# Three loads of an attention-plus-MLP kernel cut by lanes: 96 lanes and four times 8

## The chip, the cores and the metric

The kernel runs on one core of one Trainium2 chip. The metric is the device time of one execution in microseconds. The median of 3 runs of the kernel before is 282.46 us (282.33 to 282.54).

## The reference

Two steps follow each other. The attention step has no matrix of scores: `q` is put through a softmax along its 64 channels, `k` through a softmax along its 576 rows, and a 64 x 64 product of `k` and `v` stands between them.

```
q_s = softmax of q over its last axis (64 channels)     # q, k, v: (8 batches, 8 heads, 576 rows, 64), fp32
k_s = softmax of k over its rows (576)
kv  = einsum('bhsd,bhse->bhde', k_s, v)
x   = einsum('bhsd,bhde->bhse', q_s, kv)                # then (8 * 576 = 4608 tokens, 8 * 64 = 512)
h   = x @ w_in                                          # w_in: (512, 2048)
out = maximum(0.01 * h, h) @ w_out                      # w_out: (2048, 512); out: (4608, 512), fp32
```

## The kernel before, in words

**Layout.** A batch of `q`, `k` or `v` is one tile of 128 lanes by 4 head pairs by 9 rows by 64 channels (`raw`, 9,216 bytes in a lane). Lanes 0 to 63 hold one of a pair's two heads and lanes 64 to 127 the other, nine rows of the sequence in each lane. The function `load` issues such a tile, or a part of it, from SyncE's queue (L81): `cuts` lists slices of head pairs and rows, and each slice is one DMA over all 128 lanes. In one head pair, one lane has a contiguous run of 64 channels times the rows of the slice, and this run is one packet: 1,024 bytes for four rows, 1,280 for five, 1,792 for seven, 2,304 for nine.

**Stages.** The tokens are worked in nine tiles of 512. Tile 0 needs batch 0 (tokens 0 to 575), tile 1 also batch 1, and so on. In a tile, layer 1 (`layer1`, L533) makes 16 slices `ph` of the hidden layer with four matmuls each (`cb` 0 to 3, the four parts of `w_in`), ScalarE applies the leaky ReLU (`leaky`, L542), and layer 2 (`layer2`, L554) sums 16 products for each of the four groups of 128 tokens. For tile 0 layer 1 works in two halves of 256 tokens, and it begins with the slices `j` 0 to 7 (the first half of `w_in`'s columns) for `cb` 0, 1, 2, then `cb` 3, and then the slices 8 to 15 (the second half) in the same way.

**The order.** Nothing is scheduled automatically: the order of each engine is the order of the program text. Work on the next batches is hung into tile `t` at point `u` by `at(t, u, ...)` and run there by `run(t, u)`. Semaphore waits are put in by the framework. A DMA from SyncE uses one of eight semaphores in turn, and SyncE waits before it issues a DMA until the DMA that used the same semaphore eight issues earlier has landed.

**The first loads.** SyncE issues, without a wait: the rows 0 to 3 of batch 0's `q` (`RA`), `k` in two halves, `v` in two halves, and the rows 4 to 8 of `q` (`RB`, "the late q rows", 640 KB). GpSimd issues the weights: `load_w_in(0)` once batch 0's `k` is there (L590), `load_w_in(1)` after two pieces of work (L604, L205, L244), four DMAs of 128 lanes in each (L125). Then it issues the first piece of `w_out`, and the other seven (`late_loads`) when the third DMA of `load_w_in(1)` is there (L653).

**The late q rows.** VectorE takes their maxima in `q_max(0, R1)` and `q_max(0, R2)` (L216) for rows 4 to 5 and 6 to 7, in between the steps that make `kd` of head group 1 (L404, L408). GpSimd subtracts (L278), ScalarE takes the exponentials (L286), VectorE sums and scales (L295, L302), TensorE transposes (L419). TensorE's matmuls of `attend(0, (1,), RA)` (L448), which need `kd`, stand after the first eight matmuls of layer 1.

**Batch 1.** `hold_sync(0, ...)` is a DMA of 256 bytes (L585) which SyncE issues only when the first DMA of `load_w_in(1)` has landed. Behind it in SyncE's queue stand `k` of batch 1 in two halves of two head pairs each (`H0`, `H1`, 576 KB a half) and seven rows of its `q` in two halves (448 KB a half). In `more_loads`, hung at (0, 27), ScalarE writes one element of `v`'s tile (L659), and SyncE then issues `v` in two halves. VectorE works on these in the order `k_tree(1, H0)`, `k_tree(1, H1)`, `q_max` of `H0`, `k_allmax`, `q_max` of `H1`, `k_sub` of `H1`. ScalarE works in the order `q_exp` of `H0`, `k_exp` of `H1`, `q_exp` of `H1`, the two casts of `v` (L203), `k_exp` of `H0` (L193). TensorE multiplies `k` and `v` in `kv(1, (1, 0))`, hung at (0, 44): 36 matmuls of head group 1, then 36 of head group 0 (L315). The second 36 need `k_exp` of `H0`.

Of the kernel before, what the change touches and what calls it, by code (L numbers as in the profile page):

```python
# [25 lines left out]
def kernel(  # L26
# [9 lines left out]
    nc = tc.nc  # L36
# [10 lines left out]
    P = 128  # L47
# [24 lines left out]
    def raw(name):  # L72
        return raw_pool.tile([P, HL, R, D], FP32, name=name, tag="raw")

    def load(src, b, name, cuts, t=None):
        t = raw(name) if t is None else t
        flat = src[b].rearrange("h s d -> (h s d)").rearrange(
            "(hl p r d) -> p hl r d", hl=HL, p=P, r=R
        )
        for hs, rs in cuts:  # L80
            nc.sync.dma_start(  # L81
                out=t[:, hs, rs].rearrange("p h r d -> p h (r d)"),
                in_=flat[:, hs, rs].rearrange("p h r d -> p h (r d)"),
            )
        return t

    ALLH, ALLR = slice(0, HL), slice(0, R)
    RA, RB = slice(0, 4), slice(4, R)
    R1, R2, R3 = slice(4, 6), slice(6, 8), slice(8, R)
    st = [{} for _ in range(B)]  # L90


    st[0]["q"] = load(q, 0, "q_raw", [(ALLH, RA)])
    st[0]["k"] = load(k, 0, "k_raw", [(slice(0, 2), ALLR), (slice(2, 4), ALLR)])
    st[0]["v"] = load(v, 0, "v_raw", [(slice(0, 2), ALLR), (slice(2, 4), ALLR)])
    load(q, 0, "q_raw", [(ALLH, RB)], st[0]["q"])

    zero = const_pool.tile([P, P], FP32)
    nc.gpsimd.memset(zero, 0.0)  # L99
# [474 lines left out]
    H0, H1 = slice(0, 2), slice(2, 4)  # L574
# [9 lines left out]
    def hold_sync(i, src):  # L584
        nc.sync.dma_start(out=held[:, i], in_=src)  # L585
# [59 lines left out]


    hold_sync(0, w_in_sb[0:1, 0, F - 128 : F])
    st[1]["k"] = load(k, 1, "k_raw", [(H0, ALLR), (H1, ALLR)])
    R7, RE = slice(0, 7), slice(7, R)
    st[1]["q"] = load(q, 1, "q_raw", [(H0, R7), (H1, R7)])  # L650

# [5 lines left out]
    def more_loads():  # L657
        st[1]["v"] = t = raw("v_raw")
        nc.scalar.copy(out=t[0:1, 0, 0, 0:1], in_=identf[0:1, 0:1])  # L659
        load(v, 1, "v_raw", [(H0, ALLR), (H1, ALLR)], t)  # L660
        hold_sync(1, w_out_sb[0:1, 11, 0:128])
        st[2]["k"] = load(k, 2, "k_raw", [(H0, ALLR)])
        load(q, 1, "q_raw", [(ALLH, RE)], st[1]["q"])
        load(k, 2, "k_raw", [(H1, ALLR)], st[2]["k"])
        st[2]["q"] = load(q, 2, "q_raw", [(ALLH, ALLR)])
        st[2]["v"] = load(v, 2, "v_raw", [(ALLH, ALLR)])
# [5 lines left out]
    at(0, 20, lambda: q_max(1, R7, H1), lambda: q_sub(nc.gpsimd, 1, R7, H1), lambda: k_sub(nc.vector, 1, H1))  # L672
    at(0, 20, lambda: k_sub(nc.gpsimd, 1, H0))
    at(0, 27, more_loads)
    at(0, 31, lambda: q_exp(1, R7, H0), lambda: q_sum(1, R7, H0), lambda: q_norm(1, R7, H0))
    at(0, 31, lambda: k_exp(1, H1))
# [59 lines left out]
    for t in range(3, B - 1):  # L736
        b = t + 1
# [145 lines left out]
```

## Time and profile before

| What | Value |
|---|---|
| median of 3 runs | 282.46 us (282.33 to 282.54) |
| the profiled execution | 282.55 us, of which the span of instructions is 280.8 us |
| granted TensorE clock | 0.999 |
| TensorE (PE) busy | 273.7 us, 97% of the span |
| VectorE (DVE), ScalarE (ACT), GpSimd (POOL) busy | 158.9, 160.4, 47.4 us |
| DMA | 45.93 MB: SyncE's queue 41.30 MB, GpSimd's queue 4.20 MB |

PE is TensorE's matmuls and PEld its weight loads, which run beside them. The page divides the span into slices and gives each engine's busy share in tenths; the chain of work that ended last says which piece of work released the next one, from the end back to the start. The timeline lists an engine's instructions in order of time with the idle time in front of each and what ended it. An engine that is idle costs nothing unless another one waits for what it does next.

### The profile page before, as it was taken

To read this page: it belongs to the slowest core of one execution; us is meant where nothing else is said; L and a number is where in the kernel's file an instruction comes from. 1 tells how busy PE (TensorE), PEld (TensorE's weight loads), DVE (VectorE), ACT (ScalarE), POOL (GpSimd) and SP (SyncE) were. 2 spreads that over 40 slices of the span, in tenths; PEclk is the share of its full clock that TensorE was granted. 3 is DMA by queue.
4 is the path that set the end of the run, shared out by engine and by line. 5 is a ranking of instruction groups with operands and counts; after the bars stand their busy time and mean duration, and the time that the engine had idled before them with its cause. 6 is when DMAs were issued, how large, how long until landed. Compare 5 with 4: busy or idle time off the path is not lost.

```text
span 280.8 us, 4909 instructions
## 1 busy us (share of the span) xinstructions
PE 273.7 (97%) x1970; PEld 133.6 (48%) x1970; DVE 158.9 (57%) x227; ACT 160.4 (57%) x284; POOL 47.4 (17%) x52
## 2 busy tenths in 40 slices
PE   8799999999999999999999999999999999999994
PEld 3478645444444544444444444444444444444443
DVE  3984898999999949956695598644600000000021
ACT  4976565784489176755586448644844364146400
POOL 2947280158103002100300040000000000000000
PEclk9999999999999999999999999999999999999999
DMA  7999999897792599099409930333053300330033
GB/s 254 326 210 327 242 223 358 324 347 241 219 392 73 55 339 349 2 212 388 144 0 280 379 83 0 84 77 75 1 86 75 69 8 0 75 75 2 0 75 75
DMA packets 37750, 45.93 MB, mean 164 GB/s; under 512 B 16608, under 2 KB 20960, under 8 KB 37728
## 3 DMA queue, kind: packets, MB, share of 16 engines
q1 hardware_dynamic: 34240, 41.30, 47.5%
q0 software_dynamic: 3328, 4.20, 8.6%
q8 instruction: 15, 0.25, 0.4%
q10 hardware_dynamic: 160, 0.13, 0.1%
q14 instruction: 7, 0.06, 0.0%
HBM read 36.70 MB, written 9.44 MB: 164 GB/s over the span
## 4 chain that ended last, share of the span: by engine, by line
PE 91%; DMA 5%; POOL 2%; SPq 0%; issue 0%; DVE 0%
PE pout L554 45%; PE ph L533 43%; DMA w_in_sb<-in_moe_w_in_dram 3%; DMA k_raw<-in_k_dram 2%; PE po L448 1%; POOL w_in_sb L125 1%; PE pokv L315 1%; PE pkv L315 1%; POOL vb L205 0%; SPq L81 0%; POOL qe L244 0%; PE psum_q L255 0%; PE pokv L448 0%; DVE out_sb L548 0%; POOL gate L604 0%
## 5 line engine op out<-in xcount | busy, mean ns | idle before, releaser
L554 PE MATMUL pout<-w_out_sb,gj 128*128 128x512 bf16 (+2 forms) x592 | 127.9, 373 | 0.0
L533 PE MATMUL ph<-xT,w_in_sb 128*128 128x512 bf16 (+1 forms) x640 | 126.6, 358 | 0.2 <-DMA w_in_sb<-in_moe_w_in_dram 0.2
L542 ACT ACTIVATE gj<-ph 128x512 bf16<-128x512 f32 x144 | 82.0, 602 | 27.1 <-PE ph L533 26.7
L533 PEld LDWEIGHTS <-w_in_sb 128*128 128x128 bf16 x640 | 62.3, 98 | 62.4 <-DMA w_in_sb<-in_moe_w_in_dram 0.5
L554 PEld LDWEIGHTS <-gj 128*128 128x128 bf16 x592 | 56.4, 98 | 65.0 <-issue 0.2
L548 ACT COPY out_sb<-pout 128x512 f32<-128x512 f32 (+1 forms) x29 | 16.8, 581 | 67.2 <-PE pout L554 40.4
L548 DVE COPY out_sb<-pout 128x512 f32<-128x512 f32 (+1 forms) x8 | 4.8, 634 | 70.8 <-PE pout L554 70.8
L205 POOL CAST vb<-v_raw 128x1152 bf16<-128x1152 f32 x13 | 19.0, 1487 | 85.1 <-DMA v_raw<-in_v_dram 85.1
L295 DVE TENSOR_REDUCE qsum<-qe 128x36 f32<-128x2304 bf16 (+5 forms) x13 | 20.0, 1541 | 10.7 <-ACT qe L286 10.5
L193 ACT ACTIVATE ke<-k_raw 128x2304 bf16<-128x2304 f32 (+2 forms) x11 | 17.6, 1598 | 10.5 <-DVE k_raw L185 10.4
L302 DVE TENSOR_TENSOR qe<-qe,qrec 128x2304 bf16<-128x2304 bf16 (+5 forms) x13 | 21.9, 1688 | 0.4
L216 DVE TENSOR_REDUCE qmax<-q_raw 128x36 f32<-128x2304 f32 (+5 forms) x13 | 20.0, 1536 | 0.8 <-DMA q_raw<-in_q_dram 0.8
L286 ACT ACTIVATE qe<-q_raw 128x2304 bf16<-128x2304 f32 (+5 forms) x13 | 17.2, 1320 | 3.8 <-POOL q_raw L278 3.8
L185 DVE TENSOR_TENSOR k_raw<-k_raw,kall 128x2304 f32<-128x2304 f32 (+1 forms) x8 | 17.2, 2163 | 0.3
L278 POOL TENSOR_TENSOR q_raw<-q_raw,qmax 128x512 f32<-128x512 f32 (+3 forms) x7 | 11.9, 1697 | 24.0 <-DVE qmax L216 23.0
L471 ACT CAST xT<-po 128x512 bf16<-128x512 f32 (+3 forms) x34 | 15.3, 538 | 1.1 <-PE po L448 1.1
L152 DVE TENSOR_TENSOR t<-t 128x256 f32<-128x256 f32 (+2 forms) x22 | 13.9, 633 | 0.7
L278 DVE TENSOR_TENSOR q_raw<-q_raw,qmax 128x2304 f32<-128x2304 f32 (+1 forms) x6 | 13.2, 2202 | 0.3
L335 DVE RECIPROCAL krec<-pokv 128x2 f32<-128x2 f32 x8 | 1.3, 164 | 21.1 <-PE pokv L448 21.1
L152 DVE TENSOR_TENSOR t<-k_raw 128x512 f32<-128x512 f32 (+1 forms) x11 | 11.3, 1031 | 3.1 <-DMA k_raw<-in_k_dram 2.9
L347 PE MATMUL pout<-zero 128*128 128x512 f32 (+3 forms) x18 | 8.0, 561 | 1.0 <-POOL zero L99 1.0
L315 PEld LDWEIGHTS <-ke 64*64 64x64 bf16 x504 | 5.9, 107 | 3.6 <-issue 2.1
(70 smaller groups left out, 109.5 us busy)
## 6 DMA issues: line engine op xcount, KB each, us to landing
out_dram<-out_sb SPq DMA_DIRECT2D x70, 128.0 KB, 2.8
q_raw<-in_q_dram SPq DMA_DIRECT2D x6, 1152.0 KB, 8.9
v_raw<-in_v_dram SPq DMA_DIRECT2D x6, 1152.0 KB, 12.0
k_raw<-in_k_dram SPq DMA_DIRECT2D x5, 1152.0 KB, 6.6
k_raw<-in_k_dram SPq DMA_DIRECT2D x6, 576.0 KB, 5.9
v_raw<-in_v_dram SPq DMA_DIRECT2D x4, 576.0 KB, 7.5
w_in_sb<-in_moe_w_in_dram POOLq DMA_DIRECT2D x8, 256.0 KB, 7.1
w_out_sb<-in_moe_w_out_dram POOLq DMA_DIRECT2D x8, 256.0 KB, 11.1
```

Source lines behind the costliest of these rows:

```text
L152: nc.vector.tensor_tensor(out=o, in0=i0, in1=i1, op=ALU.max)
L185: eng.tensor_tensor(out=ks, in0=ks, in1=st[b]["kall"][:, hs].unsqueeze(2).to_broadcast([P, n, R, D]), op=ALU.subtract,)
L193: nc.scalar.activation(out=st[b]["ke"][:, :, hs].rearrange("p r h d -> p h r d"), in_=st[b]["k"][:, hs], func=AF.Exp,)
L205: eng.tensor_copy(out=o, in_=i)
L216: nc.vector.tensor_reduce(out=o, in_=st[b]["q"][:, hs, rs], axis=AX.X, op=ALU.max)
L278: eng.tensor_tensor(out=qs, in0=qs, in1=st[b]["qmax", rs.start, hs.start].unsqueeze(3).to_broadcast([P, m, n, D]), op=ALU.subtract,)
L295: nc.vector.reduce_sum(out=qsum, in_=st[b]["qe"][:, rs, hs], axis=AX.X)
L302: nc.vector.tensor_tensor(out=qes, in0=qes, in1=st[b]["qrec", rs.start, hs.start].unsqueeze(3).to_broadcast([P, n, m, D]), op=ALU.mult,)
L533: nc.tensor.matmul(ph, lhsT=w_in_sb[:, cb, j * P : (j + 1) * P], rhs=xT[:, cb, c0 : c0 + n], start=(cb == 0 and first), stop=(cb == NB - 1 ...
L542: nc.scalar.activation(out=o, in_=ph, func=AF.Prelu, alpha=LEAKY_SLOPE)
L548: copy(out=out_sb, in_=pout)
L554: nc.tensor.matmul(pout, lhsT=g_sb[j // 2][:, j % 2, tsub * P : (tsub + 1) * P], rhs=w_out_sb[:, j, os], start=(j == 0), stop=(j == NF - 1),)
```

## The change

`load` gets a further argument, `lanes`, a list of slices of lanes. For each cut it issues one DMA for each slice of lanes. `EVEN`, the default, is the one slice of all 128 lanes, as before. `SKEW` is five slices: lanes 0 to 95, and then 96 to 103, 104 to 111, 112 to 119 and 120 to 127. Three loads use it: the late rows of batch 0's `q`, the second half of batch 1's `k`, and the first half of batch 1's `v`. Each of them becomes five DMAs in SyncE's queue instead of one, so this queue issues twelve DMAs more. The bytes, the tiles and the packets' sizes stay the same, and so does the order of the instructions on TensorE, VectorE, ScalarE and GpSimd. An instruction that needs one of the three loads now waits for five semaphores instead of one. SyncE's turn through its eight semaphores moves on accordingly: the last two pieces of the late q rows now wait until the first two loads have landed, and the second half of batch 1's `q` until the small DMA of `hold_sync(0, ...)` has.

```diff
-    def load(src, b, name, cuts, t=None):
+    EVEN = (slice(0, P),)
+    SKEW = (slice(0, 96),) + tuple(slice(p, p + 8) for p in range(96, P, 8))
+
+    def load(src, b, name, cuts, t=None, lanes=EVEN):
         t = raw(name) if t is None else t
...
         for hs, rs in cuts:
-            nc.sync.dma_start(
-                out=t[:, hs, rs].rearrange("p h r d -> p h (r d)"),
-                in_=flat[:, hs, rs].rearrange("p h r d -> p h (r d)"),
-            )
+            for ps in lanes:
+                nc.sync.dma_start(
+                    out=t[ps, hs, rs].rearrange("p h r d -> p h (r d)"),
+                    in_=flat[ps, hs, rs].rearrange("p h r d -> p h (r d)"),
+                )
         return t
...
-    load(q, 0, "q_raw", [(ALLH, RB)], st[0]["q"])
+    load(q, 0, "q_raw", [(ALLH, RB)], st[0]["q"], SKEW)
...
-    st[1]["k"] = load(k, 1, "k_raw", [(H0, ALLR), (H1, ALLR)])
+    st[1]["k"] = load(k, 1, "k_raw", [(H0, ALLR)])
+    load(k, 1, "k_raw", [(H1, ALLR)], st[1]["k"], SKEW)
...
-        load(v, 1, "v_raw", [(H0, ALLR), (H1, ALLR)], t)
+        load(v, 1, "v_raw", [(H0, ALLR)], t, SKEW)
+        load(v, 1, "v_raw", [(H1, ALLR)], t)
```

## The prediction

> **What bounds the kernel now.** I read the chain of work that ended last first. Its second half is TensorE alone; its columns are start, duration, what.
>
> ```profile
> 13.32 8.90 DMA w_in_sb<-in_moe_w_in_dram
> 22.23 0.05 issue
> 22.27 8.91 PE ph L533 x80
> 31.18 8.63 PE pout L554 x40
> ```
>
> From 22.27 us to 277.08 us the chain names nothing but TensorE. The list of TensorE's waits after that shows how little a faster load can give back:
>
> ```profile
> PE ph L533 <- DMA w_in_sb<-in_moe_w_in_dram: 0.2, 1, 0.2
> PE pkv L393 <- ACT ke L193: 0.2, 1, 0.2
> ```
>
> The first is the only wait that a later load can cure; the second (at 12.19) is earlier than any changed load is used. The timeline gives the first as 0.24 us, at 22.27. So this kernel can gain about 0.24 us (0.09%) from better loads, and lose as much as a late load makes TensorE wait. Next, where the changed loads are used (timelines of VectorE and ScalarE):
>
> ```profile
> 14.66 0.68 DVE L216 TENSOR_REDUCE qmax<-q_raw 128x8 f32<-128x512 f32 x1
> 15.25 0.16 DVE L404 RECIPROCAL krec<-pkv 128x1 f32<-128x1 f32 x1
> ...
> 15.85 0.29 DVE L408 TENSOR_TENSOR kd<-pkv,krec 128x128 bf16<-128x128 f32 x1
> ...
> 28.40 0.69 DVE L152 TENSOR_TENSOR t<-k_raw 128x512 f32<-128x512 f32 x1 [0.17 <-DMA k_raw<-in_k_dram]
> ```
> ```profile
> 38.98 1.14 ACT L203 CAST vb<-v_raw 128x1152 bf16<-128x1152 f32 x1
> 40.54 1.15 ACT L203 CAST vb<-v_raw 128x1152 bf16<-128x1152 f32 x1 [0.42 <-DMA v_raw<-in_v_dram]
> 41.59 1.16 ACT L193 ACTIVATE ke<-k_raw 128x1152 bf16<-128x1152 f32 x1
> ```
>
> TensorE's timeline has `attend(0, (1,), RA)` at 16.26, just behind the `kd` that ends at 16.14, and `kv(1, ...)` at 42.82, whose second half starts its weight loads at 43.08; `k_exp` of `H0` ends at 42.75. Margins: 0.1 us in the first place, 0.33 us in the second. Last, what the DMA queues do with many and with few lanes (busy time by stretch; the last two figures are the share of the 16 DMA engines and GB/s):
>
> ```profile
> 5.00:9.00 4.00, 2.40 (x10) 0.75 (x10) 3.75 (x9) 3.56 (x21) 1.42 (x4) 1.00 1.04 411
> 53.00:54.00 1.00, 1.00 (x6) 0.41 (x5) 0.90 (x4) 1.00 (x3) 0.00 (x0) 1.00 1.06 407
> 240.90:242.20 1.30, 1.30 (x8) 0.59 (x7) 0.00 (x0) 0.00 (x0) 0.00 (x0) 1.00 0.83 191
> ```
>
> Loads of 128 lanes move 411 GB/s. At 53 us eight stores of 64 lanes each, of both halves of the lanes, are queued together and move 407. At 241 us only one pair of such stores is under way, the first of one half of the lanes and the second of the other, one behind the other: 191 GB/s with the DMA engines 83% busy. A 2,048-byte packet takes 84 ns in the first case and 151 ns in the second (medians of the trace's packets). So engines that all work on one half of the lanes get half the rate.
>
> **The change part by part.** The sum is made against the profiled execution, 282.55 us, of which the span is 280.8 and 1.75 lie outside; it stands 0.09 us above the median of 282.46. What I add goes onto the median.
>
> *Where the lanes go.* The trace records sixteen landings for each load, one from each DMA engine; 128 lanes are 8 on each engine. I take 96 lanes as 6 on each of sixteen, and 8 lanes as one on each of eight engines, always the same eight: those then carry 10 lanes and the other eight 6. No row shows a load of so few lanes; the nearest are the stores, 4 lanes on each of sixteen. The Trainium skill, DMA: Bandwidth & Descriptors, section Why a DMA increments its semaphore by 16 and not by 1, says that such a copy of 8 lanes is put on the eight lowest-numbered engines; no run here shows it yet.
>
> *Issue.* Twelve more DMAs on SyncE. Its timeline shows 0.46 us for an issue at the start, 1.02 at 19 to 21 us (two issues in 2.04), 0.45 at 30. The four extra of the q rows lie before the wait of `hold_sync` (SyncE idles 14.6 us there): free, as long as they are out by 18.55. The four of `k` stand ahead of batch 1's `q`, which goes out at 23.1 to 25.4 instead of 21.30. Its first half lands at 30.96, after 28.00 for fifteen of sixteen engines; a queue in front of it hides up to 2.9 us of this. The four of `v` push its second half from 30.6 to 32.4 or, at 1.02 each, 34.7; the first half's packets begin only at 33.7 (2,304-byte packets of the trace), so 0 to 1 us is exposed. I take 0 for all three.
>
> *The late q rows.* Their 1,280-byte packets start at 9.51, last at 11.7, and the load lands at 12.06, 2.6 us before VectorE's 14.66: that is the cover. From 11.2 us the weights share the engines, packet by packet, as the DMA view of 34 to 38 us shows for the same two queues:
>
> ```profile
> q1 hardware_dynamic: 365, 0.80, 58.6%
> q0 software_dynamic: 370, 0.36, 53.5%
> ```
>
> The 96-lane part alone is 480 KB: 1.2 us at 410 GB/s, or 1.7 us if its lanes 0 to 63 (327,680 bytes) go at the 191 GB/s of half the lanes. I take 1.45, so to 11.0. Each of the eight engines then has 4 lanes x 4 = 16 packets left. At the full rate one takes 55 ns. If eight engines on 8 lanes suffer as sixteen on 64 did, it takes 100; if the rate went down with the lanes (191 / 64 = 3 GB/s a lane, 41 KB in 1.7 us), about 400. I take 100, the row's own factor of two. Two or three go before the weights come; 13.5 x (0.155 + 0.10) = 3.4 us bring the last to about 14.6 (0.155 is the spacing of weight packets on an engine: eight in the 1.25 us between landings). The landing follows 0.6 us behind, hence 15.2 to 15.3 instead of 12.06. Bounds: 13.1 at the full rates, 20 at the worst. At 15.3 VectorE is 0.6 us late, `kd` is 0.6 late, TensorE waits 0.5 us at 16.26. That is in place of the 0.24 at 22.27, where TensorE now comes later than the third part of `w_in`: net +0.3 us. What else is behind the waiting VectorE instruction: GpSimd's L278 and ScalarE's L286 of the same rows, late by the same 0.6, no more.
>
> By the Trainium skill, SBUF — State Buffer, section Door 1: The DMA port swizzle, a transfer's bandwidth follows how many of 16 ports its lanes reach at about 27 GB/s each; 64 lanes of one half reach eight, and 8 adjacent lanes of this cut two. The 191 GB/s above agree for 64 lanes. By this page an 8-lane piece of the q rows would be an estimated 0.76 us, four in a row 3.0 us, and the sum of this step about +1 us instead of +0.3.
>
> *The second half of `k`.* The eight engines get 2 lanes x 2 = 4 packets of 2,304 bytes more (93 ns each) and, with the same factor, 8 packets of 0.2: up to 1.2 us later than the 26.45 at which fifteen of sixteen engines were done, 27.6. The load's last engine landed at 28.31, so VectorE's 28.40 does not move: 0. If the cover goes (landing after 28.4), `k_tree` and the chain behind it move 1:1 until `q_max`, which waits for `q` to 31.05 and leaves 0.84 us.
>
> *The first half of `v`.* Here w_out's packets share the engines until about 41 us. The eight engines have 4 more packets x (0.106 + 0.10) = 0.8 us and 8 narrow packets x 0.1 = 0.8 us: 1.6 us on 39.94, the second half's landing on thirteen of sixteen engines, gives 41.5 instead of 40.51. The cast at 40.54 goes to 41.5, `k_exp` of `H0` ends at 43.7 instead of 42.75, TensorE wants it at 43.08 + 0.3: a wait of 0.35. ScalarE issues the load behind TensorE's work, so the 0.3 moves it too: 0.65 in all. Bounds: 0 (full rate, 40.6) to 2.
>
> **Sum:** +0.3 +0.65 = +0.95, less about 0.1 for the late engine below, which may be relieved: **283.3 us**. Everything after 47 us is TensorE back to back and does not change.
>
> **The rivals.**
>
> *Relief.* From 19.78 us an instruction fetch of 16,384 bytes (1.08 us) occupies one DMA engine; the third DMA of `load_w_in(1)` has fifteen landings by 21.07 and the last at 22.23, and this is the 0.24 us wait. The same engine stays 1.3 to 3 us late in batch 1's loads (28.31 against 26.45, 30.96 against 28.00). If it is one of the eight that lose two lanes, and the narrow pieces run at full rate, it is ahead by 8 x 0.051 = 0.4 us at 22.23, the wait goes, and the others (21.07 + 0.4) are in time for 22.03. Time 282.46 - 0.24 = 282.2. For it: the lateness is one engine's, and the rest have about 1 us to spare. Against it: which engine it is no row tells, and the 191 GB/s row.
>
> *The wrong eight.* No loss by narrow lanes, but the late engine is among the eight that get two lanes more. Then 22.23 becomes 22.65 (+0.4), and `v`'s second half comes at 40.51 + 0.8 (+0.5 at TensorE): 283.4. The same rows speak for it as for relief; one even chance stands against the other.
>
> *Nothing moves.* The skewed loads arrive later, inside the cover computed above, and the late engine is not helped enough: 282.5.
>
> **How the numbers follow.** Narrow lanes slow the pieces: 0.55, of which 0.43 end above +0.2% (0.56 us, about what a measurement of this kernel can tell from no change). Relief 0.28, wrong eight 0.11 (0.08 above), nothing moves 0.06. A gain over 0.56 us would need more than the one wait of 0.24: 0.03. So slower 0.51, same 0.46, faster 0.03. The range reaches down to the relief case (282.15). Up, the q rows at 17 and `v` at 42.5 would give some 2 us: 284.7. The likeliest case's own range is 282.8 to 284.7.
>
> **What would show it.** Right: VectorE's first L216 of the late q rows waits for a q_raw DMA, TensorE's L448 near 16.3 comes late, the wait on w_in at 22.27 is gone, and L203 at 40.5 waits for v_raw longer than 0.42 us. Wrong: L216 starts at 14.66 without a wait. If also TensorE's w_in wait is gone, it was relief; if it has grown to 0.6, the wrong eight. The forecast also falls if eight engines on 8 lanes run at the full 55 and 93 ns a packet.

## The result and the profile after

The changed kernel takes 285.5 us (median of 6 runs, 284.96 to 285.93); the kernel before, in runs beside it, 282.5 us (6 runs). The ratio is 1.0104, with a 95% interval of 1.0094 to 1.0114: 3.0 us slower. The forecast was 283.3 us and at most 284.7. The direction was right; the loss is more than three times the forecast's (0.95 us, less 0.1) and outside its range. One execution, of the twelve of e10_q_gentle below, took 360.88 us at a granted clock of 0.756 and is left out of that kernel's numbers.

The profiled execution of after took 285.1 us, span 283.3 (before: 282.55 and 280.8). Lines of the changed file are 4 higher: layer 1 is L537, layer 2 L558, `kv` L319, `q_max` L220, the casts L207.

First the waits of TensorE in after (line, who released it: total us, times, longest):

```profile
PE pout L558 <- DMA w_out_sb<-in_moe_w_out_dram: 2.0, 3, 1.3
PE ph L537 <- DMA w_in_sb<-in_moe_w_in_dram: 0.3, 1, 0.3
```

The first line is new. It names `w_out`, a load that the change does not touch. TensorE's timeline of after shows where (start, duration, what, idle time in front and its releaser):

```profile
16.26 0.38 PE L452 MATMUL po<-qT,kd 64*64 64x256 bf16 x4
...
21.38 1.05 PE L537 MATMUL ph<-xT,w_in_sb 128*128 128x256 bf16 x8 [0.30 <-DMA w_in_sb<-in_moe_w_in_dram]
...
22.70 8.91 PE L537 MATMUL ph<-xT,w_in_sb 128*128 128x256 bf16 x80
...
37.22 1.89 PE L558 MATMUL pout<-w_out_sb,gj 128*128 128x512 bf16 x8 [0.43 <-DMA w_out_sb<-in_moe_w_out_dram]
40.44 1.89 PE L558 MATMUL pout<-w_out_sb,gj 128*128 128x512 bf16 x8 [1.34 <-DMA w_out_sb<-in_moe_w_out_dram]
...
42.92 2.75 PE L558 MATMUL pout<-w_out_sb,gj 128*128 128x512 bf16 x11 [0.20 <-DMA w_out_sb<-in_moe_w_out_dram]
45.60 0.78 PE L319 MATMUL pkv<-vb,ke 64*64 64x65 bf16 x72
...
50.09 5.13 PE L537 MATMUL ph<-xT,w_in_sb 128*128 128x512 bf16 x22
```

Before, the layer 2 matmuls that are the first to read `w_out`'s sixth DMA, and the first matmuls of tile 1, were:

```profile
40.14 2.75 PE L554 MATMUL pout<-w_out_sb,gj 128*128 128x512 bf16 x12
47.31 2.97 PE L533 MATMUL ph<-xT,w_in_sb 128*128 128x512 bf16 x13
```

`attend` begins at 16.26, as before: the late q rows, which land at 14.71, don't make TensorE wait. The 80 matmuls begin at 22.70 instead of 22.27 (+0.43). Layer 2 of tile 0 then waits three times for `w_out`, 1.97 us in all. Tile 1 begins at 50.09; before, the same matmuls begin at 47.31 (+2.78). After that TensorE is back to back, and the ends differ by 2.55 us. The chain of work that ended last runs through DMA where TensorE alone stood before (start, duration, what):

```profile
13.19 9.38 DMA w_in_sb<-in_moe_w_in_dram
23.15 2.86 POOL w_out_sb L134 x4
26.00 16.88 DMA w_out_sb<-in_moe_w_out_dram
42.92 1.02 PE pout L558 x4
```

The second line of it is late by itself: GpSimd issues the last seven DMAs of `w_out` from 23.15 us, 0.34 us later than before (22.81), since it waits for `w_in` first.

Where the changed loads are read, after (VectorE's and ScalarE's timelines):

```profile
14.79 0.69 DVE L220 TENSOR_REDUCE qmax<-q_raw 128x8 f32<-128x512 f32 x1 [0.16 <-issue]
...
31.38 0.69 DVE L156 TENSOR_TENSOR t<-k_raw 128x512 f32<-128x512 f32 x1 [1.78 <-DMA k_raw<-in_k_dram]
```
```profile
42.96 1.15 ACT L207 CAST vb<-v_raw 128x1152 bf16<-128x1152 f32 x1 [0.27 <-DMA v_raw<-in_v_dram]
44.13 1.16 ACT L197 ACTIVATE ke<-k_raw 128x1152 bf16<-128x1152 f32 x1
```

The second half of `k` is read 3 us later than before (31.38 for 28.40), the second half of `v` 2.4 us later (42.96 for 40.54). Neither shows as a wait of TensorE: `k_exp` ends at 45.29, and `kv` at 45.60 is itself late by then.

Last, what the DMA engines moved while `k` was loaded; the last two figures of a row are their busy share and GB/s. Before, then after:

```profile
25.00:26.00 1.00, 1.00 (x12) 0.89 (x11) 0.00 (x0) 1.00 (x4) 1.00 (x2) 1.00 1.04 401
26.00:27.00 1.00, 1.00 (x12) 0.90 (x10) 0.64 (x1) 1.00 (x4) 1.00 (x2) 1.00 1.08 389
```
```profile
25.00:26.00 1.00, 1.00 (x12) 0.89 (x10) 0.00 (x0) 1.00 (x3) 1.00 (x2) 1.00 1.07 253
26.00:27.00 1.00, 1.00 (x12) 0.90 (x10) 0.00 (x0) 1.00 (x3) 1.00 (x3) 1.00 1.06 263
```

The engines are as busy as before and move a third less. From 22 to 30 us they move 2.11 MB instead of 2.63. Of what is missing, 0.13 MB falls before 24 us, as `k` is issued 1.2 us later; the other 0.38 MB, while the pieces are loaded, is 0.95 us of work at 400 GB/s. The next load behind `k` and `q` on the same engines is `w_out`. Its second DMA lands at 31.83 instead of 29.93. TensorE's three waits end with its fourth, fifth and sixth, which land at 37.18, 40.40 and 42.88 (before 34.30, 37.14 and 40.10). For the sixth TensorE had no margin before: it landed at 40.10 and was used at 40.14.

### The profile page after: what moved, and what is told of

Same layout as the page of the kernel before. It is cut to its first block, busy times and chain, and to the rows that moved or that the text cites. A ratio compares the mean times of both kernels' runs of the same rounds, so it can differ in the third digit from the quotient of the medians.

```text
span 283.3 us, 4905 instructions
## 1 busy us (share of the span) xinstructions
PE 274.1 (97%) x1943; PEld 134.0 (47%) x1970; DVE 159.4 (56%) x227; ACT 160.5 (57%) x284; POOL 50.0 (18%) x52
## 4 chain that ended last, share of the span: by engine, by line
PE 83%; DMA 13%; POOL 1%; issue 1%; ACT 0%; SPq 0%; DVE 0%; ACTq 0%; POOLq 0%
PE pout L558 41%; PE ph L537 39%; DMA w_out_sb<-in_moe_w_out_dram 6%; DMA w_in_sb<-in_moe_w_in_dram 3%; DMA q_raw<-in_q_dram 3%; DMA k_raw<-in_k_dram 2%; PE po L452 1%; POOL w_out_sb L134 1%; PE pokv L319 1%; PE pkv L319 1%; ACT gj L546 0%; SPq L85 0%; PE psum_q L259 0%; PE pokv L452 0%; DVE out_sb L552 0%
## 5 line engine op out<-in xcount | busy, mean ns | idle before, releaser
L558 PE MATMUL pout<-w_out_sb,gj 128*128 128x512 bf16 (+2 forms) x575 | 127.0, 373 | 3.1 <-DMA w_out_sb<-in_moe_w_out_dram 2.0
L537 PE MATMUL ph<-xT,w_in_sb 128*128 128x512 bf16 (+1 forms) x630 | 126.2, 357 | 0.8 <-DMA w_in_sb<-in_moe_w_in_dram 0.3
L537 PEld LDWEIGHTS <-w_in_sb 128*128 128x128 bf16 x640 | 62.1, 98 | 63.2 <-DMA w_in_sb<-in_moe_w_in_dram 1.2
L558 PEld LDWEIGHTS <-gj 128*128 128x128 bf16 x592 | 56.4, 98 | 67.4 <-issue 2.9
L209 POOL CAST vb<-v_raw 128x1152 bf16<-128x1152 f32 x13 | 21.5, 1682 | 82.5 <-DMA v_raw<-in_v_dram 82.5
L220 DVE TENSOR_REDUCE qmax<-q_raw 128x36 f32<-128x2304 f32 (+5 forms) x13 | 20.0, 1537 | 0.6 <-DMA q_raw<-in_q_dram 0.4
L156 DVE TENSOR_TENSOR t<-t 128x256 f32<-128x256 f32 (+2 forms) x22 | 16.4, 743 | 0.7
L282 POOL TENSOR_TENSOR q_raw<-q_raw,qmax 128x512 f32<-128x512 f32 (+3 forms) x7 | 11.9, 1697 | 26.7 <-DVE qmax L220 25.4
L475 ACT CAST xT<-po 128x512 bf16<-128x512 f32 (+3 forms) x34 | 15.3, 538 | 1.6 <-PE po L452 1.6
L351 PE MATMUL pout<-zero 128*128 128x512 f32 (+3 forms) x18 | 9.4, 645 | 1.0 <-POOL zero L103 1.0
L319 PEld LDWEIGHTS <-ke 64*64 64x64 bf16 x504 | 5.8, 107 | 3.7 <-issue 2.5
```

The costliest lines, as they stand in the source:

```text
L156: nc.vector.tensor_tensor(out=o, in0=i0, in1=i1, op=ALU.max)
L209: eng.tensor_copy(out=o, in_=i)
L220: nc.vector.tensor_reduce(out=o, in_=st[b]["q"][:, hs, rs], axis=AX.X, op=ALU.max)
L282: eng.tensor_tensor(out=qs, in0=qs, in1=st[b]["qmax", rs.start, hs.start].unsqueeze(3).to_broadcast([P, m, n, D]), op=ALU.subtract,)
L537: nc.tensor.matmul(ph, lhsT=w_in_sb[:, cb, j * P : (j + 1) * P], rhs=xT[:, cb, c0 : c0 + n], start=(cb == 0 and first), stop=(cb == NB - 1 ...
L558: nc.tensor.matmul(pout, lhsT=g_sb[j // 2][:, j % 2, tsub * P : (tsub + 1) * P], rhs=w_out_sb[:, j, os], start=(j == 0), stop=(j == NF - 1),)
```

## The experiments

Times are medians; "before" is the kernel before in runs beside them (medians of 282.46 to 282.60 us). Each diff is against the changed kernel unless it says otherwise.

### One part alone: late q rows (e1_q_only)

```diff
-    load(k, 1, "k_raw", [(H1, ALLR)], st[1]["k"], SKEW)
+    load(k, 1, "k_raw", [(H1, ALLR)], st[1]["k"])
...
-        load(v, 1, "v_raw", [(H0, ALLR)], t, SKEW)
+        load(v, 1, "v_raw", [(H0, ALLR)], t)
```

> Only the late q rows are cut as in the changed kernel; k and v of batch 1 are loaded as before. Narrow lanes: this load alone puts eight engines 1.3 us behind, so the second half of w_in is 1.2 us later for them and SyncE's small DMA, which waits for it, goes out at 19.8 instead of 18.55. TensorE's stalls around w_in (0.4 us) stay, and w_out, which stands behind w_in on the same engines, is 1.3 us late instead of 2.9: 283.4-284.2. If k and v carry the loss, 282.5-282.9. If the q rows carry all of it, 285 or more.

283.29 us against 282.56, ratio 1.0023 (1.0013 to 1.0032): +0.7 us. TensorE's timeline:

```profile
17.02 0.39 PE L537 MATMUL ph<-xT,w_in_sb 128*128 128x256 bf16 x2 [0.41 <-DVE kd L412]
...
21.07 1.05 PE L537 MATMUL ph<-xT,w_in_sb 128*128 128x256 bf16 x8 [0.41 <-DMA w_in_sb<-in_moe_w_in_dram]
```

The rows land at 15.80 here and at 14.71 in the kernel after, so in one execution TensorE waits for `kd` and in the other it doesn't. In both there is a wait for `w_in`, longer than before, but for an earlier part of it: the first DMA of its second half here (landed at 21.03), the second in after (21.33), where before it was the third (22.23). The engines that loaded the narrow pieces bring `w_in` late too: in after, the sixteen landings of the first DMA of its second half come in two groups, seven by 18.38 and nine from 19.19 to 19.76 (before, all from 17.98 to 18.54). The wait itself is made by the very last of the sixteen: in after the other fifteen of the second DMA are there by 20.98, 0.1 us before TensorE wants it. Why one engine is later still isn't shown.

### The other two parts alone: k and v (e2_kv_only), k (e6_k_only), v (e7_v_only)

```diff
-    load(q, 0, "q_raw", [(ALLH, RB)], st[0]["q"], SKEW)
+    load(q, 0, "q_raw", [(ALLH, RB)], st[0]["q"])
```

e6_k_only also takes `SKEW` from `v`, e7_v_only from `k`.

> Only the second half of batch 1's k and the first half of its v are cut as in the changed kernel; the late q rows are loaded as before. Narrow lanes: w_in is as before (third DMA at 22.2, TensorE's wait 0.24 us), then w_out falls behind by 1.0-1.6 us on the loaded engines, and TensorE waits for w_out in layer 2 of tile 0: 283.3-284.3. If the q rows carry the loss: 282.5.

> Only the second half of batch 1's k is skewed. Theory (the loaded engines fall behind in w_out, which lies on the same engines behind k and v): k's 8-lane packets at 25 to 28 us push w_out's second DMA from 29.93 to 31 or later and TensorE waits 1 to 1.5 us for w_out in its layer 2 of tile 0: 283.6 to 284.0, more than half of the 2.3 us of e2_kv_only, since v's first half begins too late (its packets at 33.7) to cause the first of e2's waits at 37.8. Rival (v, which shares the engines with w_out longest, is the cause): k costs at most 0.3, 282.5 to 282.8.

> Only the first half of batch 1's v is skewed. Theory (k sets w_out back first, v adds): w_out's fifth and sixth DMA come up to 1 us late, v's second half lands at 41.5, cast and k_exp are late by about 1: TensorE loses 0.4 to 1 us, 282.9 to 283.5. Rival (v is the cause of e2_kv_only's loss): 284.4 or more, with 1.5 us of waits on w_out or more. If k alone and v alone together cost much less than 2.3 us, the two share one slack, which each alone doesn't use up.

`k` and `v`: 284.90 us, ratio 1.0085 (1.0069 to 1.0101), +2.3, where I had expected 284.3 at most. With the q rows' 0.7 this is the whole 3.0. `k` alone: 283.72, ratio 1.0053 (1.0037 to 1.0069), +1.3. `v` alone: 283.95, ratio 1.0048 (1.0034 to 1.0062), +1.5. The timelines, first of e6_k_only, then of e7_v_only:

```profile
38.55 1.89 PE L558 MATMUL pout<-w_out_sb,gj 128*128 128x512 bf16 x8 [0.58 <-DMA w_out_sb<-in_moe_w_out_dram]
```
```profile
42.66 1.15 ACT L207 CAST vb<-v_raw 128x1152 bf16<-128x1152 f32 x1 [1.33 <-DMA v_raw<-in_v_dram]
```
```profile
43.87 0.48 PE L319 MATMUL pkv<-vb,ke 64*64 64x65 bf16 x36 [0.52 <-ACT vb L207]
44.94 0.48 PE L319 MATMUL pkv<-vb,ke 64*64 64x65 bf16 x36 [0.59 <-ACT ke L197]
```

The two lose by different ways. `k` sets `w_out` back (second DMA at 31.36). The profiled execution of e6_k_only is the fastest of its four (283.10 us), so its wait of 0.58 us shows about half of the median's 1.3. `v` comes late itself (its second half lands at 42.64), and `kv` waits 1.1 us for cast and `k_exp`; the list of waits names no `w_out`. I had expected 0.4 to 1 us of this. With both, the new waits are for `w_out` alone (2.2 us in e2_kv_only), and the late `v` hides behind them.

### Spread pieces, and a spread load (e3_stride, e4_count)

e3_stride takes every fourth lane of 96 to 127 for each small piece, so each is still 8 lanes. e4_count cuts the load into five pieces that put the same number of lanes on every engine, 64 lanes and four times 16.

```diff
-    SKEW = (slice(0, 96),) + tuple(slice(p, p + 8) for p in range(96, P, 8))
+    SKEW = (slice(0, 96),) + tuple(slice(96 + i, P, 4) for i in range(4))   # e3_stride
+    SKEW = (slice(0, P, 2),) + tuple(slice(i, P, 8) for i in range(1, 8, 2))   # e4_count
```

> The same three loads in five DMAs each, 96 lanes and four times 8, so every DMA engine carries the same number of lanes as in the changed kernel (10 or 6 by my count). Only the 8 lanes of a piece are now every fourth lane from 96 to 127 instead of 8 neighbours. Narrow lanes (eight engines writing 8 neighbouring lanes hinder each other): the 8-lane packets of 1,280 bytes go back from 146-148 ns to about 55, the late q rows land near 13.5 instead of 14.7, the weights' landings of the eight loaded engines come 0.4 us behind the others instead of 1.3, and the time falls from 285.5 to 282.2-282.9. Uneven engines (10 lanes against 6 is itself the cause): the loaded engines stay as late as in the changed kernel, 285 or more. Count (twelve more DMAs, their issues and waits): 285 or more.

> The same three loads in five DMAs each again, but even: one DMA of 64 lanes (every second lane) and four of 16 lanes (every eighth), each spread over all 128 lanes. By my count every engine carries 4 + 4 x 1 = 8 lanes, as before the change. Count: 285 or more, since the DMAs, the issues and the waits of the changed kernel are all there. Narrow lanes and uneven engines: within 0.4 us of before, 282.2-282.9, with the late engine of before (its w_in landing at 22.23, TensorE's wait of 0.24 us) as it was.

e3_stride: 284.68 us, ratio 1.0082 (1.006 to 1.0104). The q rows' small packets take 86 ns instead of 148, but `k`'s 2,304-byte packets still 140 to 165 (medians by microsecond, 25 to 28 us), so narrow neighbours can't be the main price: 2.1 of the 3.0 us stay, between the two ranges that I had expected. e4_count: 283.33, ratio 1.0032 (1.0019 to 1.0046), no wait for weights at all, but 0.8 us slower than before, more than the 0.4 that I had allowed. What it loses is SyncE's time (timelines of SyncE and ScalarE):

```profile
30.12 4.72 SPq L85 DMA_DIRECT2D v_raw<-in_v_dram  x6
```
```profile
41.75 1.15 ACT L207 CAST vb<-v_raw 128x1152 bf16<-128x1152 f32 x1 [1.06 <-DMA v_raw<-in_v_dram]
```

Six issues of `v`, five of them with spread lanes, take 4.72 us (2.18 in after): 0.58 to 0.66 us each, and one 1.47. So the second half is late and `kv` waits 0.6 us for `k_exp`.

### Two pieces: 96 and 32, or even and odd (e9_96_32, e11_even_odd)

Up to here I took the uneven share of the engines (ten lanes on eight of them, six on the others) as the cause. These two cut each load in two, with an even share in both.

```diff
-    SKEW = (slice(0, 96),) + tuple(slice(p, p + 8) for p in range(96, P, 8))
+    SKEW = (slice(0, 96), slice(96, P))   # e9_96_32
+    SKEW = (slice(0, P, 2), slice(1, P, 2))   # e11_even_odd
```

> All three loads of the change as two DMAs, lanes 0 to 95 and lanes 96 to 127: the cut stays, the four 8-lane pieces are one piece of 32 lanes. Theory (what costs is the share of the eight engines that take every 8-lane piece): 96 and 32 lanes are 6 and 2 on each of sixteen engines, an even load; w_out's second DMA lands near 30.0 and its sixth by 40.2, TensorE doesn't wait for w_out, v's second half lands near 41: 282.4 to 282.9. Rival (a load cut at lane 96 is slow in itself, since a piece covers only a part of the lanes): the packets of the 32-lane piece take 100 ns or more in place of 55 and 150 or more in place of 93, the engines fall behind w_out all the same, and TensorE waits 0.5 us or more in layer 2 of tile 0: 283.3 to 284.5.

> All three loads of the change as two DMAs, the even lanes and the odd lanes: as many DMAs as in e9_96_32 and the same even share of the engines, but each DMA reaches over the whole of the 128 lanes. Theory (in e9_96_32 the packets were slow, 148 ns in place of 93, because each piece covers only one stretch of neighbouring lanes): the packets of k's second half cost about 93 to 106 again, w_out's second DMA lands by 30.2, no wait on w_out: 282.5 to 283.0. Rival (cutting a load in two costs that, wherever the cut lies): packets of 140 or more, w_out's fifth DMA at 38 or later in place of 37.1, a wait of 0.6 or more: 283.4 to 283.9.

e9_96_32: 283.63 us, ratio 1.005 (1.0033 to 1.0066). e11_even_odd: 282.63, ratio 1.001 (0.9997 to 1.0022), no difference from before. So a loss doesn't need an uneven share. TensorE's wait in e9_96_32, and the DMA rows of e9_96_32 and of e11_even_odd:

```profile
39.25 1.89 PE L558 MATMUL pout<-w_out_sb,gj 128*128 128x512 bf16 x8 [0.91 <-DMA w_out_sb<-in_moe_w_out_dram]
```
```profile
25.00:26.00 1.00, 1.00 (x11) 0.89 (x10) 0.00 (x0) 1.00 (x3) 1.00 (x3) 1.00 1.08 297
26.00:27.00 1.00, 1.00 (x12) 0.90 (x10) 0.00 (x0) 1.00 (x4) 1.00 (x2) 1.00 1.08 255
```
```profile
25.00:26.00 1.00, 1.00 (x11) 0.90 (x10) 0.00 (x0) 1.00 (x3) 1.00 (x2) 1.00 1.05 409
26.00:27.00 1.00, 1.00 (x12) 0.88 (x10) 0.94 (x2) 1.00 (x3) 1.00 (x3) 1.00 1.09 370
```

As many DMAs, the same bytes, the same share: 255 to 297 GB/s with neighbouring lanes, 370 to 409 with alternate ones. In e9_96_32, 197 of `k`'s packets from 22 to 30 us take over a quarter longer than 93 ns (median of these 152); in e11_even_odd none. The 32-lane piece has only 64 packets, so most of the slow ones belong to the 96-lane piece or to `k`'s first half beside it.

For `k` an even share is enough to lose most of it. From 24 to 30 us e9_96_32 moves 0.29 MB less than before and e6_k_only, with the uneven share, 0.40 MB less: 0.7 and 1.0 us of work at 400 GB/s. In e9_96_32 all sixteen landings of `w_out`'s second DMA are late alike, 30.85 to 31.20 (29.63 to 29.93 before); about 0.5 us of this is there when `w_in` ends, from the late q rows. In e6_k_only six come by 30.33 and ten from 30.90 to 31.36.

This isn't the whole 3.0 us: e9_96_32 loses 1.0. What the four 8-lane pieces add isn't divided between their uneven share, their narrowness and their number. `v` needs them: in e9_96_32 its packets, in turn with those of `w_out`, take 106 ns as before, and its second half lands at 40.70 (40.51 before, 42.64 in e7_v_only).

### The same uneven share, lanes spread (e12_k_spread)

Against e6_k_only:

```diff
-    SKEW = (slice(0, 96),) + tuple(slice(p, p + 8) for p in range(96, P, 8))
+    SKEW = (slice(0, P, 2), slice(1, P, 4)) + tuple(
+        slice(p, P, 16) for p in (3, 7, 11, 15)
+    )
```

> Only the second half of batch 1's k, with the share of the change (ten lanes on eight engines, six on the others) but lanes spread over all 128: every second lane, every fourth, and four pieces of eight lanes, every sixteenth. Theory (the lanes that a piece covers set most of the price, the uneven share the rest): packets near 93 to 110 in place of 160 to 182, w_out's second DMA lands by 30.5 in place of 31.36, and TensorE waits at most 0.2 for w_out: 282.5 to 283.1. Rival (the uneven share is what costs in e6_k_only): w_out's second DMA at 31 or later and a wait of 0.5 or more: 283.4 to 284.0. Seven issues of k take up to 5 us of SyncE, so batch 1's q rows come later; a wait of VectorE for them past 31.05 would be a cost of its own.

283.62 us, ratio 1.0041 (1.0025 to 1.0057): as slow as e6_k_only, for another reason. SyncE's and TensorE's timelines (this file's lines are 2 higher again):

```profile
19.59 5.42 SPq L87 DMA_DIRECT2D k_raw<-in_k_dram  x7
25.06 1.31 SPq L87 DMA_DIRECT2D q_raw<-in_q_dram  x2
```
```profile
40.73 0.55 PE L261 MATMUL psum_q<-ident,qe 128*128 128x128 bf16 x7 [0.80 <-ACT qe L292]
```

No packet of `k` is slow, `w_out`'s second DMA lands at 28.23, and there is no wait for `w_out`. The loss is what the expectation named as a cost of its own: seven issues, of 0.57 to 0.72 us and one of 1.45, push batch 1's `q` to 25.06 us (21.30 before). The test is not clean: pieces issued that slowly may not have lain in the queue together, so what an uneven share costs in a full queue stays open.

### The late q rows with less skew (e5_q_stride, e10_q_gentle)

Only the late q rows, against the kernel before: e5_q_stride with the pieces of e3_stride, e10_q_gentle with

```diff
+    SKEW = (slice(0, 112), slice(112, P, 2), slice(113, P, 2))
```

> Only the late q rows are skewed, and their four 8-lane pieces take every fourth lane of 96 to 127 instead of eight neighbours. Theory (the same eight engines carry two more lanes each, and neighbours are slow besides): the 1,280-byte packets cost about 86 ns as in e3_stride, the q rows land near 14.1, before VectorE wants them at 14.66, so the wait of 0.41 at kd that e1_q_only showed is gone. The two groups of engines in w_in's third DMA lie 0.9 us apart, and the engine that fetches instructions is among the relieved ones, so TensorE's wait on w_in is at most 0.3: 282.2 to 282.7. Rival (the slow part of e1_q_only is the uneven share alone, whichever lanes the pieces take): the rows land at 15 or later, TensorE waits 0.4 at kd again: 283.1 to 283.4.

> Only the late q rows, as 112 lanes and two loads of 8 lanes, every second lane of 112 to 127: 9 lanes on eight engines and 7 on the others, half the skew of e5_q_stride. If relief of the engine that fetches instructions is worth its 0.24 us at all, it shows here: that engine is 0.2 us ahead (22.0 in place of 22.23) and the loaded ones, 0.2 to 0.4 us behind 21.07, still come before TensorE wants w_in at 22.03, so the wait on w_in is gone: 282.2 to 282.4. If the fetch costs what it cost before wherever it falls, or the loaded engines take its place as in e5_q_stride, a wait of 0.2 to 0.45 on w_in stays: 282.4 to 282.7.

e5_q_stride: 282.60 us against 282.46, ratio 1.0006 (0.9996 to 1.0016); the rows land at 14.12, the wait at `kd` is gone, the one for `w_in` is 0.45 us. e10_q_gentle: 282.71 against 282.60, ratio 1.0012 (1.0001 to 1.0023); no wait for `w_in` is left, and the time is no better. That wait is absent in e11_even_odd and e6_k_only as well, which don't relieve any engine ahead of `w_in`, so its absence isn't proof of relief either.

### w_out queued earlier (e8_wout_early)

```diff
-        nc.gpsimd.tensor_copy(out=gate[:, 0:1], in_=w_in_sb[:, 2, F - 1 : F])
+        nc.gpsimd.tensor_copy(out=gate[:, 0:1], in_=w_in_sb[:, 0, F - 1 : F])
```

> The kernel after, but GpSimd's gate ahead of the last seven DMAs of w_out waits for the first part of w_in instead of the third, so those DMAs are queued 2 to 3 us earlier. All skewed loads stay. Theory (the loss from 31 to 48 us is w_out coming late for layer 2 of tile 0): w_out lands earlier by 1 to 3 us, TensorE's waits on w_out shrink from 2.0 to under 0.7, and batch 1's k, q or v become later instead: 283.5 to 284.3. Rival (the loss comes from the late v or from a TensorE that is late in any case): 285 or more, with w_out's waits gone and another in their place.

288.22 us, ratio 1.0216 (1.0177 to 1.0255). My expectation of 283.5 to 284.3 was wrong by 4 us. The waits of TensorE:

```profile
PE psum_q L259 <- ACT qe L290: 2.4, 1, 2.4
PE ph L537 <- DMA w_in_sb<-in_moe_w_in_dram: 0.8, 2, 0.6
```

`w_out` isn't waited for any more, but `w_in` and batch 1's `q` are: the lateness moves to whoever stands behind in the queues. The last DMA of `w_out` lands at 45.17, as late as in after (45.42; 42.66 before, 42.19 in e11_even_odd). So an earlier place in the queue doesn't bring it earlier. From 25 to 30 us `k`'s packets, in turn with those of `w_out`, take 106 ns (median), and the engines move 278 to 295 GB/s: the slow packets are gone, and so is the stretch of about 400 GB/s that `k` had to itself before.

Part of the loss is TensorE's clock. After the wait of 2.4 us the granted clock is 0.79 from 43 to 44 us, 0.50 to 0.51 from 44 to 47 and 1.00 again from 47, and four matmuls of layer 2 take 1.91 us instead of 1.04:

```profile
43.53 0.89 PE L259 MATMUL psum_q<-ident,qe 128*128 128x128 bf16 x7 [2.45 <-ACT qe L290]
44.21 1.91 PE L558 MATMUL pout<-w_out_sb,gj 128*128 128x512 bf16 x4
```

TensorE is busy for about 3 us of this time, so half speed costs an estimated 1.5 us. In after, a wait of 1.34 us left the clock at 1.00. What the earlier gate does to the kernel before was not tried.

## Why the prediction was wrong in size

- *TensorE is the bound, and a gain is at most 0.24 us.* Held: none of the kernels beat the kernel before.
- *Issue costs nothing.* Held for after: `k`'s six issues took 2.85 us, and `q` went out at 23.33, inside the forecast's 23.1 to 25.4. With spread lanes an issue takes about 0.6 to 0.75 us, and the same step would have failed (e4_count, e12_k_spread).
- *Late q rows, +0.3.* Measured alone +0.7. The landing was near (15.80 and 14.71 for 15.3), the wait at `kd` too where it came (0.41 for 0.5). The term that failed is the credit of 0.24: a wait for `w_in` didn't go but grew, to 0.41 in e1_q_only and 0.30 in after, since earlier parts of `w_in` came late enough to be waited for, behind the same engines' narrow pieces and one engine that was later still. My packet price of 100 ns, the halves' factor of two, was too low: 148 ns in after. By the Trainium skill, SBUF — State Buffer, section Door 1: The DMA port swizzle, the prediction put this step at an estimated +1, and the run's 0.7 lies between the two. With 0.19 us a packet, its estimate from that section, in place of 0.10, the prediction's own sum would have been 1.2 us longer, an estimated +1.5.
- *Second half of `k`, 0.* Measured alone +1.3: the step that failed most, a term put at nothing. I left the 96-lane part at the full rate and slowed only the narrow packets, so I had the load at 27.6; alone it lands at 28.90 and is read at 28.98. That much the reader's 0.84 us of slack hides, as the step said. But I asked only who reads `k`: the loss came through `w_out`, queued on the same engines, which the forecast prices nowhere. In after `k` is read at 31.38, as SyncE's `hold_sync` waits for `w_in` and goes out at 19.78 instead of 18.55: a second way in which one late load delays the next that the forecast left out.
- *First half of `v`, +0.65.* The mechanism was right, and the term was mis-sized: 1.5 us alone. Fifteen engines had the second half by 41.81, near the forecast's 41.5, and the narrow packets took 207 to 218 ns beside `w_out`, as priced (106 and 100). The sixteenth landed at 42.64. I had counted from 39.94, the thirteenth engine, and credited 0.1 for a late engine relieved; in e7_v_only the late one is among the loaded eight. The cast was forecast for 41.5 and ran at 42.66. In after all this is covered by the waits for `w_out`.
- *The rivals.* All three left the lost rate out, and none gives the measured time. On which eight the late engine falls changes with the execution: in after among the relieved (the early group of `w_in`'s landings shrinks from seven to six behind the instruction fetch), in e7_v_only's `v` among the loaded. So neither rival could be read off the profile before, and both, priced at 0.9 us or less, fall short of the 3.0.
- *The signs that it named.* In after VectorE waits only 0.16 us for the late q rows, `attend` isn't late, and the second cast of `v` waits 0.27 us, less than the 0.42 of before. The third part of `w_in` is no longer waited for, but an earlier one is. So the forecast's own story was not what cost the time in after.
- *What the prediction's own row held.* It quoted 191 GB/s for stores of one half of the lanes and used it for the first 64 lanes of the late q rows only. The same 64 lanes lead the 96-lane parts of `k` and `v`.

What the lanes have to do with the rate is not shown beyond the numbers. By the Trainium skill, SBUF — State Buffer, section Door 1: The DMA port swizzle, lanes 0 to 63 and 64 to 127 lie on eight ports each, and 32 of a half reach as many as its 64. By this the 96-lane piece fills one eight as long as a whole load does (an estimated 1.35 us for `k` at 27.2 GB/s a port), and the 32-lane piece comes on top with an estimated 0.68 us. The trace of e9_96_32 agrees: from 24 to 30 us it moves 0.29 MB less than before, 0.7 us at 400 GB/s. Alternate lanes reach all ports by the same section, and they lost nothing in e11_even_odd.

## What to carry to other kernels

When a load is slowed, price everything that is queued behind it on the DMA engines, not only its reader: here `w_out`, with 0.04 us of margin, paid for `k`. Before a load is cut by lanes, look for a row with part of the lanes. Here pieces of neighbouring lanes cost a third of the rate while no `w_out` ran beside `k`, and two such pieces of `v`, beside `w_out`, cost next to nothing (its second half landed at 40.70 for 40.51). Alternate lanes kept the rate, but each spread piece took about 0.6 to 0.75 us of its queue's issue time. A slack that looks free at TensorE has to be checked at the second link (weights behind activations), since parts that lose alone by different waits can cover each other when they stand together.

## What the hardware showed that I had not expected

- The time of a packet depends on which lanes its DMA covers: 2,304 bytes take 93 ns in a load of 128 lanes or of every second lane, and 144 to 148 (medians) while lanes 0 to 95 and 96 to 127 are loaded; 1,280 bytes take 55 ns, or 148 in 8 neighbouring lanes, or 86 in 8 lanes four apart. In turn with packets of `w_out` the 2,304 bytes take 106 in a load of 128 lanes and in one of 96 and 32 alike (e9_96_32, `v`).
- The busy share doesn't show it: 1.06 to 1.07 at 253 to 263 GB/s, against 1.04 to 1.08 at 389 to 401.
- A DMA of 8 lanes leaves nine landings in the trace instead of sixteen, one at once and eight with the data: it uses eight engines.
- An issue from SyncE takes 0.27 to 0.43 us for 8 neighbouring lanes in after, and mostly 0.59 to 0.77 us for a piece with spread lanes in e3_stride, e4_count and e12_k_spread. In these two last and in before, one issue of batch 1's loads takes 1.4 to 1.5 us, in before one of 128 lanes; why isn't shown.
- After TensorE had waited 2.4 us in e8_wout_early, the granted clock was about 0.50 for some 3 us.
